# Weight decoding, attention factors and range checks moved to other steps in a fused RWKV and two-MLP kernel

## The chip, the cores and the metric

One core of a Trainium2 chip runs the whole program. The metric is the device time in microseconds (us), the median of three runs. The engines are named as in the profile: PE (TensorE) multiplies matrices, PEld is its weight load, DVE (VectorE), ACT (ScalarE) and POOL (GpSimd) work on elements, and SP issues the DMAs of this program. Each engine takes its instructions in the order in which the program lists them, so an instruction that waits holds up all that stand behind it on that engine.

## The reference

The input goes through a linear attention and then through two MLPs, all of it in float32:

```python
for t in range(S):                       # S = 768, per batch (4) and head (8), D = 48
    cur = einsum('bhd,bhe->bhde', u * kt, vt)
    y[:, :, t] = einsum('bhd,bhde->bhe', rt, state + cur)
    state = wt[..., None] * state + einsum('bhd,bhe->bhde', kt, vt)
x = y.transpose(0, 2, 1, 3).reshape(3072, 384)
h = x @ w_in;  g = h * clip(h + 3, 0, 6) / 6;  x = g @ w_out     # d_ff 2048
out = (x @ w_a) * (x @ w_b) @ w_out2                             # d_ff 1536
```

## The kernel before

The sequence is cut into 6 blocks of 128 positions; with 4 batches that makes 24 attention units (unit n is block n // 4, batch n % 4) and 6 token blocks of 512 tokens for the MLPs. Each fp32 product in the MLPs is made of three matmuls on rounded high and low parts (`mm3`, L471), so each operand is split into a high part (a rounding copy on ACT) and a low part (a subtraction on DVE).

Two hand-written schedules set the order. A list of tokens (`CFG["start"]`) runs units 0 to 7 and the first half (8 of 16 weight tiles) of the first layer for token block 0. Then `run` (L819 and on) goes through numbered steps s. Steps 8 to 95 are the rest of the first MLP: one step is one weight tile of one token block. Steps 8 to 15 are tiles 0 to 7 for block 1, steps 16 to 23 tiles 8 to 15 for block 0, steps 24 to 31 tiles 8 to 15 for block 1; then each of the blocks 2 to 5 has 16 steps. Steps 96 to 167 are the second MLP, 12 for each block; there the step is also counted as sb = s - 96.

In a step of the first MLP the engines get, in this order: the attention's element work that is due (`att_ew`, L378), the first product `h` on PE (`L1_pe`, L499) into one of two PSUM banks in turn, relu (`t`, L510, ACT), its product with h (`t<-t,h`, L514, DVE: below "mul"), `gh` (L518, ACT), `gl` (L523, DVE), the first decoding operation (L418, ACT), the split of the weight tile that was decoded two steps earlier (`w`: L462 on ACT, L465 on DVE), the second product `x2a` of step s - 2 on PE (`L2_pe`, L534), the rest of the decoding, then the attention's matmuls, its loads (`att_loads`, L396), and the loads and splits of the second MLP's input. Where a part of the first MLP ends (steps 7, 15, 23, ...), `L2_pe` also copies the three banks of `x2a` out: banks 0 and 2 on ACT (L560), bank 1 on DVE (L558). The next part's `x2a` writes the same three banks and waits for those copies.

**Decoding.** The weights come as 64-bit numbers. Tile i is loaded into `raw` (two buffers, 768 KB each; the copies of `x2a` take the same two buffers in turn) and made into fp32 by two scalings on ACT (L418, L427), a shift and a mask on DVE (L432, L436) and two additions on POOL (L443). `CFG["dec"]` names the steps in which tiles 8 to 15 are decoded; `w_step2` issues the load of the next tile right behind a tile's decoding. Tile f of these is needed by `h` at step f + 8. The second MLP's tiles are decoded at steps 80 to 104, one a step from step 94 on.

**Attention.** A unit goes through stages on consecutive steps. Stage 0 is `z` (L184), `c` (L192, L193), `s` (L197) and `k` (L206) on DVE: two scans of the decay, and the product of r and k with the factors (the "factor operation"). Stage 1 has PE transpose k (`T`, L251) and form r times k (`A`, L272); stage 3 has `Y` (L339), which reads r for the last time. `load_rkw` (L133) of unit n + 2 stands in stage 1 and fills the buffer of unit n, so SP waits there for unit n's `Y`. Units 8 to 11 (block 2) start at steps 17, 20, 23 and 26.

**Checks.** `check_load` and `check_unit` (L696, L702) reload each unit's decay and test its range: four operations on DVE (L707, L708, L709, L712), one unit on every second step from sb = 1 on. `check_sum` (L726) at sb = 62 adds the result up, and the program reads it at its end.

**Second MLP.** In each step `ab` (L475, two products into a pair of banks), `ta` on ACT (L597) and DVE (L598), `ph` (L601), `pl` (L602), and `oa` (L620) of step sb - 2. Its input comes back from DRAM (`x2_load`); for blocks 0 and 1 two halves are added (L576) and then split (L577 on ACT, L578 on DVE), all in `x2_split`. Block 1's loads stand in sb = 3, 5 and 7, and its splits in sb = 5, 7 and 9.

Of the kernel before, what the change touches and what calls it, by code (L numbers as in the profile page):

```python
# [12 lines left out]
ALU = mybir.AluOpType  # L13
# [6 lines left out]
NBLK = S // 128  # L20
NF1 = 16
NF2 = 12
# [16 lines left out]
    "off": (0, 3, 6, 9),  # L39
    "stage": (0, 1, 2, 3, 4, 5, 0, 2),  # L40
    "second": (17, 20, 23, 26),
    "dec": (10, 11, 13, 14, 16, 17, 19, 20),
    "late": (-16, -14, -12, -10, -8, -6, -4, -2, -1, 0, 1, 2, 3, 4, 5, 6, 7, 8),
    "heat": 13,
    "pool": (
# [27 lines left out]
def rwkv_moe_kernel(ctx: ExitStack, tc: tile.TileContext, rkw, nat, vst, wall, ub, ud, cst, out):  # L73
    nc = tc.nc
# [13 lines left out]
    x2p = [dr.tile([3, 128, 512], F32, name=f"x2p{j}", tag=f"x2p{j}") for j in range(2)]  # L88
# [30 lines left out]
    units = [(j, b) for j in range(NBLK) for b in range(B)]  # L119
# [13 lines left out]
    def load_rkw(n):  # L133
        j, b = units[n]
        if n in FIRST:
            t = spare([128, 1024], f"rkw{n}")
        else:
            t = ap_.tile([128, 1545], F32, name=f"rkw{n}", tag="rkw")
            U[n]["w"] = t[:, 1024:1545]
        if n == 0 or n in FIRST:  # L140
            nc.sync.dma_start(out=U[n]["w"], in_=rkw[b, j, :, 1024:1545])
            nc.sync.dma_start(out=t[:, 0:1024], in_=rkw[b, j, :, 0:1024])
        else:
            nc.sync.dma_start(out=t, in_=rkw[b, j])
        if 0 < n < N_DOT:
            get_nat(n)
        U[n]["rkw"] = t
# [7 lines left out]
    def load_nat(n):  # L155
        j, b = units[n]
        c = slice(2 * DM if n < N_DOT else 0, 3 * DM)
        nc.sync.dma_start(out=get_nat(n)[:, c], in_=nat[b, j, :, c])

    def load_vs(n):  # L160
        j, b = units[n]
        nc.sync.dma_start(out=U[n]["vs"], in_=vst[b, j].rearrange("p (a c d) -> p a c d", a=NP, c=2))
# [3 lines left out]
    def get_xT(j, nm):  # L166
        if (j, nm) not in xT:
            h = gp.tile([128, 3, 512], F32R, name=f"xh_{nm}{j}", tag="xh", bufs=2)
            l = gp.tile([128, 3, 512], F32R, name=f"xl_{nm}{j}", tag="xl", bufs=2)
            xT[(j, nm)] = (h, l)  # L170
        return xT[(j, nm)]
# [206 lines left out]
    def att_ew(n, stage):  # L378
        j = units[n][0]
        for a in {  # L380
            0: "zcsk", "d0": "d", "d1": "oO", 1: "u" if j else "", 2: "tm",
            3: "efh" if j < NBLK - 1 else "ef", "x": "x", 5: "HL",
        }.get(stage, ""):
            atom[a](n)
# [9 lines left out]
                nc.tensor.matmul(out=o, lhsT=wz[:, 0:128], rhs=wz, start=True, stop=True)  # L394

    def att_loads(n, stage):  # L396
        if stage == 1 and n + 2 < len(units):
            load_rkw(n + 2)
        elif stage == 3 and n + 2 < len(units):
            load_vs(n + 2)  # L400
        elif stage == 4 and n + 3 < len(units):
            load_nat(n + 3)

    raw = {}
# [94 lines left out]
    def L1_pe(s):  # L499
        (_, j, f, _, _), c0, c1 = part(s)  # L500
        h = bank(3 + slot(s) % 2, None, f"h{s}")[:, 0:c1 - c0]
        hb[s] = h
        xh, xl = xT[(j, "a")]
        w = W[f]
        mm3(h, [((w[:, 0, k * 128:(k + 1) * 128], w[:, 1, k * 128:(k + 1) * 128]), (xh[:, k, c0:c1], xl[:, k, c0:c1])) for k in range(3)])
# [20 lines left out]
    def L1_ew(s):  # L526
        L1_relu(s)
        L1_mul(s)

    def L1_ew2(s):  # L530
        L1_high(s)
        L1_low(s)
# [30 lines left out]
    def x2_load(j, k):  # L563
        e = gp.tile([128, 512], F32, name=f"x2r{j}_{k}", tag="t", bufs=3)
        nc.sync.dma_start(out=e, in_=x2d[j][k])
        raw["x2", j, k] = e
        if raw.get("parts") and j < 2:
            e = ap_.tile([128, 3 * DM], F32, name=f"x2q{j}_{k}", tag="nat", bufs=3)[:, 0:512]
            nc.sync.dma_start(out=e, in_=x2p[j][k])
            raw["x2p", j, k] = e  # L570

    def x2_split(j, k):
        h, l = get_xT(j, "b")
        e = raw.pop(("x2", j, k))
        if ("x2p", j, k) in raw:
            nc.vector.tensor_tensor(out=e, in0=e, in1=raw.pop(("x2p", j, k)), op=ALU.add)  # L576
        nc.scalar.copy(out=h[:, k], in_=e)  # L577
        nc.vector.tensor_tensor(out=l[:, k], in0=e, in1=h[:, k].bitcast(F32), op=ALU.subtract)  # L578

# [2 lines left out]
    def L3_pe(s):  # L582
        j, f = divmod(s, NF2)
        xh, xl = xT[(j, "b")]
        w = W[NF1 + f]
        r = []
        for q in range(2):
            o = bank((3, 4, 6, 7)[2 * (s % 2) + q], None, f"ab{s}_{q}")
            c = q * 384
            mm3(o, [((w[:, 0, c + k * 128:c + (k + 1) * 128], w[:, 1, c + k * 128:c + (k + 1) * 128]), (xh[:, k], xl[:, k])) for k in range(3)])  # L590
            r.append(o)
        ab[s] = r
# [48 lines left out]
    for n in range(FIRST_N, len(units)):  # L641
        j, i = divmod(n, 4)
        n0 = CFG["second"][i] if j == 2 else NF1 * (j - 1) + CFG["off"][i]
        a, b, c, d, x, h, d0, d1 = (n0 + k for k in CFG["stage"])
# [45 lines left out]
            w_ahead()  # L690

    UNITS = len(units)
    CHECK = max(NF2 * (NBLK - 1) + 2, 2 * UNITS + 4)
    chk = {}

    def check_load(n):  # L696
# [122 lines left out]
    def run(at, first, ew, fast):  # L819
        lag, end = [max(first - 1, 0), 0], NA + NBLK * NF2 - 1  # L820
        for s in range(first, end + 1):
            act = at.get(s, [])
            sb = s - NA
            for n, sg in act:
                ew(n, sg)
            if 0 <= s < NA:
                L1_pe(s)
            elif 0 <= sb < NBLK * NF2:
                L3_pe(sb)
            if 0 <= s < NA:  # L830
                L1_ew(s)
                L1_ew2(s)
            elif 0 <= sb < NBLK * NF2:
                L3_ew(sb)
            w_step1(s)
            w_step(s)
            while lag[0] <= min(s - 2, NA - 1):
                L2_pe(lag[0])
                lag[0] += 1
            while lag[1] <= (sb - 2 if s < end else sb):  # L840
                L4_pe(lag[1])
                lag[1] += 1
            if fast and sb == CHECK:
                check_sum()
            w_step2(s)
            for n, sg in act:
                att_pe(n, sg)
            if fast:
                for n, sg in act:
                    att_loads(n, sg)  # L850
                c, r = divmod(sb - 1, 2)
                if r == 0 and 0 <= c <= UNITS:
                    if c:
                        check_unit(c - 1)
                    if c < UNITS:
                        check_load(c)
                    else:
                        check_all()
            for j in range(NBLK):
                base = NA + NF2 * j - (12 if j else 13)  # L860
                for k in range(3):
                    if s == base + 3 + 2 * k:
                        x2_load(j, k)
                    if s == base + 5 + 2 * k:
                        x2_split(j, k)

# [110 lines left out]
```

## Time and profile before

| | |
|---|---|
| median of 3 runs | 1033.86 us (1032.52 to 1036.76) |
| the profiled execution | 1032.36 us |
| its span, first to last instruction | 1030.6 us, so 1.76 us lie around it |
| PE busy | 992.9 us (96%), 7135 matmuls |
| PE weight load busy | 816.9 us (79%) |
| DVE, ACT, POOL busy | 593.8 us (58%), 347.5 us (34%), 125.2 us (12%) |
| mean granted clock of PE | 0.986 |

The shares are means over very different stages. A table by stretch shows where PE stands idle, the timeline of PE shows which instruction it waited in front of, and the timelines of the other engines show what that instruction's releaser was doing. The granted clock is 1.00 at PE's upper level of 2.4 GHz and 0.50 at 1.2 GHz; a mean in between is a mixture of the two.

### The profile page before, as it was taken

How to read it: one execution, taken by the hardware profiler on the slowest of the kernel's cores; microseconds unless marked ns; L12 is line 12 of the kernel's file. 1: busy time of each engine (PE TensorE's matmuls, PEld its weight loads, DVE VectorE, ACT ScalarE, POOL GpSimd, SP SyncE). 2: the span in 40 equal slices, each digit the busy share in tenths (PEclk: the TensorE clock that was granted, in tenths of full speed). 3: DMA queues.
4: the chain of work that ended last, by engine and by line, in shares of the span. 5: the costliest groups of instructions: out<-in, count | busy, mean ns of one | idle time of the engine just before them, and what ended most of it. 6: DMA issues, size and time to landing. Idle time of an engine off the chain costs nothing.

```text
span 1030.6 us, 16913 instructions
## 1 busy us (share of the span) xinstructions
PE 992.9 (96%) x7135; PEld 816.9 (79%) x7135; DVE 593.8 (58%) x916; ACT 347.5 (34%) x582; POOL 125.2 (12%) x118
## 2 busy tenths in 40 slices
PE   8998977999999999999999997999999999999997
PEld 4776865777778788787887876888888888888886
DVE  8998687657655765663666677444444444322222
ACT  4364643333323323233556543222222222222211
POOL 1220243211211120210233331000000000000000
PEclk9999988999999999999999998999999999999999
DMA  7363432241321321220343441110110110100001
GB/s 280 126 232 130 161 104 89 85 135 65 110 99 57 101 86 65 90 101 1 102 145 121 160 157 43 56 50 30 62 42 22 62 41 21 52 11 1 32 1 34
DMA packets 30037, 86.64 MB, mean 84 GB/s; under 512 B 3456, under 2 KB 10880, under 8 KB 29952
## 3 DMA queue, kind: packets, MB, share of 16 engines
q1 hardware_dynamic: 29664, 85.37, 24.3%
q8 instruction: 58, 0.95, 0.4%
q14 instruction: 27, 0.22, 0.1%
q10 hardware_dynamic: 288, 0.10, 0.0%
HBM read 74.45 MB, written 11.01 MB: 83 GB/s over the span
## 4 chain that ended last, share of the span: by engine, by line
PE 43%; issue 33%; DVE 9%; POOL 6%; ACT 3%; DMA 2%; SPq 0%; POOLq 0%; ACTq 0%; DVEq 0%
PE ab L475 26%; PE oa L620 13%; DMA raw<-in_wall_dram 2%; POOL wa L443 2%; PE h L475 2%; PE x2a L544 1%; DVE w L465 1%; POOL nat L216 1%; POOL nat L215 1%; POOL nat L240 1%; DVE raw L436 1%; ACT raw L418 1%; DVE t L514 1%; DVE wa L432 1%; ACT w L462 1%
## 5 line engine op out<-in xcount | busy, mean ns | idle before, releaser
L475 PE MATMUL ab<-xh_b,w 128*128 128x512 f32 x864 | 227.4, 398 | 8.2 <-ACT w L462 5.9
L475 PEld LDWEIGHTS ab<-xh_b,w 128*128 128x128 f32 x864 | 162.3, 189 | 43.1 <-ACT w L462 6.2
L475 PE MATMUL h<-xh_a,w 128*128 128x512 f32 x576 | 159.0, 410 | 3.1 <-ACT w L462 1.3
L544 PE MATMUL x2a<-gh,w 128*128 128x512 f32 x576 | 154.9, 400 | 6.5 <-ACT x2e L560 6.1
L598 DVE TENSOR_TENSOR ta<-ab,ta 128x512 f32<-128x512 f32 x72 | 49.7, 690 | 190.6 <-PE ab L475 190.6
L544 PEld LDWEIGHTS x2a<-gh,w 128*128 128x128 f32 x576 | 108.9, 190 | 33.1 <-ACT x2e L560 6.5
L475 PEld LDWEIGHTS h<-xh_a,w 128*128 128x128 f32 x576 | 104.6, 190 | 29.0 <-DVE w L465 2.8
L475 PE MATMUL ab<-xl_b,w 128*128 128x512 f32 x432 | 124.8, 397 | 0.0
L510 ACT ACTIVATE t<-h,half 128x512 f32<-128x512 f32 x96 | 66.0, 688 | 156.3 <-PE h L475 156.2
L620 PE MATMUL oa<-w,ph 128*128 128x384 f32 x576 | 113.5, 338 | 0.0
L514 DVE SCALAR_TENSOR_TENSOR t<-t,h 128x512 f32<-128x512 f32 x96 | 65.6, 683 | 78.7 <-ACT t L510 78.7
L620 PEld LDWEIGHTS oa<-w,ph 128*128 128x128 f32 x576 | 103.1, 188 | 6.0
L523 DVE TENSOR_TENSOR gl<-t,gh 128x512 fp32r<-128x512 f32 x95 | 71.5, 753 | 60.6 <-ACT gh L518 60.6
L518 ACT CAST gh<-t 128x512 fp32r<-128x512 f32 x96 | 59.6, 621 | 123.7 <-DVE t L514 123.7
L475 PEld LDWEIGHTS ab<-xl_b,w 128*128 128x128 f32 x432 | 81.9, 189 | 20.1
L601 ACT CAST ph<-ta 128x512 fp32r<-128x512 f32 x72 | 44.7, 620 | 157.3 <-DVE ta L598 157.3
L597 ACT COPY ta<-ab 128x512 f32<-128x512 f32 x72 | 42.2, 586 | 159.0 <-PE ab L475 159.0
L443 POOL TENSOR_TENSOR wa<-wa,raw 128x384 int32<-128x384 int32 x59 | 68.4, 1179 | 223.8 <-DVE raw L436 174.8
L544 PE MATMUL x2a<-gl,w 128*128 128x512 f32 x288 | 85.9, 398 | 0.0
L602 DVE TENSOR_TENSOR pl<-ta,ph 128x512 fp32r<-128x512 f32 x72 | 54.8, 762 | 49.4 <-ACT ph L601 49.4
L475 PE MATMUL h<-xl_a,w 128*128 128x512 f32 x288 | 83.2, 397 | 0.0
L544 PEld LDWEIGHTS x2a<-gl,w 128*128 128x128 f32 x288 | 54.6, 190 | 13.6 <-DVE gl L523 0.3
(88 smaller groups left out, 1028.7 us busy)
## 6 DMA issues: line engine op xcount, KB each, us to landing
raw<-in_wall_dram SPq DMA_DIRECT2D x34, 768.0 KB, 4.6
rkw<-in_rkw_dram SPq DMA_DIRECT2D x21, 772.5 KB, 4.4
nat<-in_nat_dram SPq DMA_DIRECT2D x16, 576.0 KB, 3.9
cw<-in_rkw_dram SPq DMA_DIRECT2D x24, 260.5 KB, 2.8
x2d<-x2e SPq DMA_DIRECT2D x18, 256.0 KB, 2.4
x2r<-x2d SPq DMA_DIRECT2D x18, 256.0 KB, 3.0
out_dram<-oe SPq DMA_DIRECT2D x24, 192.0 KB, 2.0
vs<-in_vst_dram SPq DMA_DIRECT2D x22, 192.0 KB, 4.6
```

The lines of the kernel that those rows point to most:

```text
L443: eng.tensor_tensor(out=a[:, c], in0=a[:, c], in1=t[:, c, 0], op=ALU.add)
L475: nc.tensor.matmul(out=o, lhsT=lt, rhs=rt, start=(i == 0), stop=(i == 3 * n - 1))
L510: nc.scalar.activation(out=t, in_=hb[s], func=ACTF.Relu, bias=half, scale=1.0 / 6.0)
L514: nc.vector.scalar_tensor_tensor(out=t, in0=t, scalar=1.0, in1=hb.pop(s), op0=ALU.min, op1=ALU.mult)
L518: nc.scalar.copy(out=gh, in_=G["t", s])
L523: ve(f"l{s}").tensor_tensor(out=gl, in0=G.pop(("t", s)), in1=G[s][0].bitcast(F32), op=ALU.subtract)
L544: nc.tensor.matmul(out=acc1[i][k][:, c0:c1], lhsT=w[:, e, 384 + k * 128:512 + k * 128], rhs=rt, start=(first and e == 0 and rt is gh), sto ...
L597: nc.scalar.copy(out=t, in_=a)
L598: nc.vector.tensor_tensor(out=t, in0=bb, in1=t, op=ALU.mult)
L601: nc.scalar.copy(out=gh, in_=t)
L602: nc.vector.tensor_tensor(out=gl, in0=t, in1=gh.bitcast(F32), op=ALU.subtract)
L620: nc.tensor.matmul(out=acc2[j][b][:, 0:384], lhsT=lt[:, b * 128:(b + 1) * 128], rhs=rt, start=(f == 0 and rt is wh and lt is ph), stop=(la ...
```

## The change

Tiles 8 to 15 are decoded at steps 9 to 16, one a step. The factor operation `k` goes from stage 0 to stage 1, ahead of `u` (L309), and the load of unit n + 2's r, k and w goes from stage 1 to stage 3. The checks start at sb = 12 and end at sb = 60. The addition of the two halves of x2 becomes a function of its own and stands one step ahead of the split.

```diff
-    "dec": (10, 11, 13, 14, 16, 17, 19, 20),
+    "dec": (9, 10, 11, 12, 13, 14, 15, 16),
...
-            0: "zcsk", "d0": "d", "d1": "oO", 1: "u" if j else "", 2: "tm",
+            0: "zcs", "d0": "d", "d1": "oO", 1: "ku" if j else "k", 2: "tm",
...
-        if stage == 1 and n + 2 < len(units):
+        if stage == 3 and n + 2 < len(units):
             load_rkw(n + 2)
-        elif stage == 3 and n + 2 < len(units):
             load_vs(n + 2)
...
+    def x2_sum(j, k):
+        if ("x2p", j, k) in raw:
+            e = raw["x2", j, k]
+            nc.vector.tensor_tensor(out=e, in0=e, in1=raw.pop(("x2p", j, k)), op=ALU.add)
+
     def x2_split(j, k):
         h, l = get_xT(j, "b")
         e = raw.pop(("x2", j, k))
-        if ("x2p", j, k) in raw:
-            nc.vector.tensor_tensor(out=e, in0=e, in1=raw.pop(("x2p", j, k)), op=ALU.add)
...
-    CHECK = max(NF2 * (NBLK - 1) + 2, 2 * UNITS + 4)
+    CHECK = max(NF2 * (NBLK - 1) + 2, 2 * UNITS + NF2 + 2)
...
-                c, r = divmod(sb - 1, 2)
+                c, r = divmod(sb - NF2, 2)
...
+                    if s == base + 4 + 2 * k:
+                        x2_sum(j, k)
```

Three places show what moves. The first is ACT in steps 9 to 11, where `x2e0` are the copies of the first part's banks and `raw8` is weight tile 8. Before, from step 9's `gh` on:

```order
L518 CAST gh9_1439<-t9_1436 128x512
L560 COPY x2e0_1452<-x2a0_0_860 128x512
L560 COPY x2e0_1452<-x2a0_2_862 128x512
L510 ACTIVATE t10_1469<-h10_1459,half_85 128x512
L518 CAST gh10_1472<-t10_1469 128x512
L418 ACTIVATE raw8_1407<-raw8_1407 128x768
L427 ACTIVATE raw8_1407<-raw8_1407 128x768
L510 ACTIVATE t11_1507<-h11_1497,half_85 128x512
```

The same place after the change:

```order
L517 CAST gh9_1439<-t9_1436 128x512
L417 ACTIVATE raw8_1407<-raw8_1407 128x768
L559 COPY x2e0_1453<-x2a0_0_860 128x512
L559 COPY x2e0_1453<-x2a0_2_862 128x512
L426 ACTIVATE raw8_1407<-raw8_1407 128x768
L509 ACTIVATE t10_1478<-h10_1468,half_85 128x512
L517 CAST gh10_1481<-t10_1478 128x512
L417 ACTIVATE raw9_1466<-raw9_1466 128x768
L426 ACTIVATE raw9_1466<-raw9_1466 128x768
L509 ACTIVATE t11_1516<-h11_1506,half_85 128x512
```

Tile 8's first scaling now stands ahead of the two bank copies, and tile 9's in step 10, ahead of step 11's relu.

The second is DVE where unit 8 begins (step 17): `zp8`, `pc8`, `seed` are `z`, `c` and `s`, the operation that writes `rkw8` is `k`, and `x2e1` is the copy of the second part's bank 1. Before:

```order
L436 SCALAR_TENSOR_TENSOR raw12_1632<-raw12_1632 128x768
L184 SCALAR_TENSOR_TENSOR zp8_1701<-rkw8_1268,ones_rev_87 128x520
L192 TENSOR_SCALAR pc8_1703<-zp8_1701 128x8
L193 RECIPROCAL seed_88<-pc8_1703 128x8
L197 SCALAR_TENSOR_TENSOR zp8_1701<-rkw8_1268,seed_88 128x519
L206 TENSOR_TENSOR rkw8_1268<-rkw8_1268,zp8_1701 128x1024
L514 SCALAR_TENSOR_TENSOR t17_1720<-t17_1720,h17_1710 128x512
L523 TENSOR_TENSOR gl17_1725<-t17_1720,gh17_1723 128x512
L558 COPY x2e1_1737<-x2a1_1_1478 128x512
L432 TENSOR_SCALAR wa13_1745<-raw13_1699 128x768
```

After the change:

```order
L435 SCALAR_TENSOR_TENSOR raw15_1694<-raw15_1694 128x768
L184 SCALAR_TENSOR_TENSOR zp8_1732<-rkw8_1268,ones_rev_87 128x520
L192 TENSOR_SCALAR pc8_1734<-zp8_1732 128x8
L193 RECIPROCAL seed_88<-pc8_1734 128x8
L197 SCALAR_TENSOR_TENSOR zp8_1732<-rkw8_1268,seed_88 128x519
L513 SCALAR_TENSOR_TENSOR t17_1750<-t17_1750,h17_1740 128x512
L522 TENSOR_TENSOR gl17_1755<-t17_1750,gh17_1753 128x512
L464 TENSOR_TENSOR w14_1757<-wa14_1689,w14_1757 128x768
L557 COPY x2e1_1769<-x2a1_1_1487 128x512
L206 TENSOR_TENSOR rkw8_1268<-rkw8_1268,zp8_1732 128x1024
```

What stands ahead of unit 8 is now the mask of the last tile (15) instead of tile 12's, `k` stands behind step 17's products, and no decoding follows.

The third is DVE in sb = 5 and 6 of the second MLP (`raw32`, `raw26` are weight tiles, `cw1` is a unit's decay under check, `x2r1_0` the first third of block 1's input). Before:

```order
L436 SCALAR_TENSOR_TENSOR raw32_5939<-raw32_5939 128x768
L707 TENSOR_REDUCE chk_m_5879<-cw1_5884 128x1
L708 TENSOR_REDUCE chk_m_5879<-cw1_5884 128x1
L709 SCALAR_TENSOR_TENSOR cw1_5884<-cw1_5884,ones_rev_87 128x520
L712 COPY chk_p_5878<-cw1_5884 128x8
L576 TENSOR_TENSOR x2r1_0_5886<-x2r1_0_5886,x2q1_0_5888 128x512
L578 TENSOR_TENSOR xl_b1_5999<-x2r1_0_5886,xh_b1_5998 128x512
L598 TENSOR_TENSOR ta6_6027<-ab6_1_6017,ta6_6027 128x512
```

After the change:

```order
L435 SCALAR_TENSOR_TENSOR raw32_5929<-raw32_5929 128x768
L580 TENSOR_TENSOR xl_b1_5984<-x2r1_0_5876,xh_b1_5983 128x512
L600 TENSOR_TENSOR ta6_6011<-ab6_1_6001,ta6_6011 128x512
L604 TENSOR_TENSOR pl6_6015<-ta6_6011,ph6_6014 128x512
L464 TENSOR_TENSOR w25_6019<-wa25_5924,w25_6019 128x768
```

The four check operations are gone from between the mask and step 6's product, and the addition has gone to the step before.

## Rows read from the trace of the kernel before

**Rows 1.** Windows: us, PE, PEld, DVE, ACT, POOL busy (count), PEclk, DMA share, GB/s

```profile
33.00:39.00 6.00, 4.80 (x62) 3.10 (x63) 5.97 (x10) 1.37 (x6) 2.09 (x2) 0.72 0.26 99
169.00:186.00 17.00, 9.66 (x87) 7.28 (x87) 9.39 (x16) 6.68 (x10) 4.90 (x5) 0.70 0.13 50
618.90:631.60 12.70, 6.57 (x21) 4.80 (x20) 9.68 (x14) 5.87 (x9) 3.21 (x3) 0.73 0.19 62
203.00:553.00 350.00, 350.00 (x3051) 279.77 (x3051) 217.01 (x355) 126.66 (x202) 51.40 (x51) 1.00 0.26 90
646.40:1023.00 376.60, 376.60 (x1793) 327.95 (x1792) 142.98 (x226) 82.34 (x141) 0.00 (x0) 1.00 0.10 32
```

**Rows 2.** PE timeline: start us, us, what, count [idle before <-releaser]

```profile
135.54 1.56 PE L475 MATMUL h<-xh_a,w 128*128 128x512 f32 x6
139.76 1.57 PE L475 MATMUL h<-xh_a,w 128*128 128x512 f32 x6
148.09 2.50 PE L544 MATMUL x2a<-gh,w 128*128 128x512 f32 x5 [6.06 <-ACT x2e L560]
175.44 1.98 PE L272 MATMUL A<-rkw 48*64 48x64 f32 x32 [5.40 <-DVE nat L349]
```

**Rows 3.** DVE and ACT timelines at step 17; SP's waits from 160 to 170 us

```profile
139.53 1.23 DVE L184 TENSOR_TENSOR_SCAN zp<-rkw,ones_rev 128x520 f32<-128x520 f32 x1
143.69 1.83 DVE L206 TENSOR_TENSOR rkw<-rkw,zp 128x1024 f32<-128x1024 f32 x1
145.44 0.68 DVE L514 SCALAR_TENSOR_TENSOR t<-t,h 128x512 f32<-128x512 f32 x1
147.47 1.05 ACT L560 COPY x2e<-x2a 128x512 f32<-128x512 f32 x2
...
SPq L144 <- PE Y L339: 11.6, 1, 11.6
```

**Rows 4.** DVE, ACT, POOL and SP timelines, a decoding at step 13 and behind

```profile
121.76 0.69 DVE L514 SCALAR_TENSOR_TENSOR t<-t,h 128x512 f32<-128x512 f32 x1 [0.55 <-ACT t L510]
126.88 0.68 DVE L514 SCALAR_TENSOR_TENSOR t<-t,h 128x512 f32<-128x512 f32 x1
123.01 0.90 ACT L418 ACTIVATE raw<-raw 128x768 f32<-128x768 f32 x1
127.04 2.04 POOL L443 TENSOR_TENSOR wa<-wa,raw 128x384 int32<-128x384 int32 x2 [7.24 <-DVE raw L436]
129.10 4.32 SPq L410 DMA_DIRECT2D raw<-in_wall_dram  x2
```

**Rows 5.** Tile raw from 88 to 200 us, and SP's issue of tile 8

```profile
DMA to landing us min/median/max: 4.2/4.2/8.1
99.60 0.46 SPq L410 DMA_DIRECT2D raw<-in_wall_dram  x1
```

**Rows 6.** PE timeline of the second MLP's first steps, columns as in rows 2

```profile
566.38 1.57 PE L475 MATMUL ab<-xh_b,w 128*128 128x512 f32 x6
606.15 1.67 PE L475 MATMUL ab<-xh_b,w 128*128 128x512 f32 x6 [1.72 <-ACT ta L597]
624.94 0.79 PE L475 MATMUL ab<-xh_b,w 128*128 128x512 f32 x1 [5.86 <-ACT w L462]
646.36 1.57 PE L475 MATMUL ab<-xh_b,w 128*128 128x512 f32 x6
652.70 1.56 PE L475 MATMUL ab<-xh_b,w 128*128 128x512 f32 x6
```

**Rows 7.** DVE timeline there: a check, an addition, two products

```profile
601.08 0.69 DVE L707 TENSOR_REDUCE chk_m<-cw 128x1 f32<-128x521 f32 x1
604.28 0.68 DVE L576 TENSOR_TENSOR x2r<-x2r,x2q 128x512 f32<-128x512 f32 x1
606.25 0.68 DVE L598 TENSOR_TENSOR ta<-ab,ta 128x512 f32<-128x512 f32 x1
611.57 0.69 DVE L598 TENSOR_TENSOR ta<-ab,ta 128x512 f32<-128x512 f32 x1
```

## The prediction, written before the changed kernel ran

> **What bounds the kernel now.** I read the table by stretch first. From 203 to 553 us and from 646 to 1023 us PE is busy for the whole stretch at a granted clock of 1.00, its 2.4 GHz level [rows 1]: nothing that other engines do faster there can shorten the run. What can be won lies in the rows of that table in which PE is not full, 169 to 186 us and 618.9 to 631.6 us, and in the two waits of PE's timeline that are nearest to them. So I took PE's timeline next, for the instruction that waited and its releaser, then the timelines of DVE, ACT and SP, for what the releaser had been doing.
>
> First stall: the first `x2a` of step 16 waits 6.06 us, until 148.09, for ACT's copies of the part before [rows 2]. ACT makes them behind step 17's `gh`, and that needs step 17's mul on DVE, which stands behind unit 8's `z`, `c`, `s` and `k` [rows 3]. Second stall: at 175.44 `A` of unit 9 had waited 5.40 us for a bank that DVE frees [rows 2]; DVE stood behind the decoding of tile 15, whose load SP issued late, since it stood for 11.6 us at the load of unit 10 until unit 8's `Y` was done [rows 3]. Third: in the second MLP's first steps PE waits 1.72 us for `ta` and 5.86 us for a weight split [rows 6], while DVE does decoding, a check and an input addition in one step [rows 7].
>
> **The checks and the addition.** Steps sb = 2 to 13 ran from 566.38 to 652.70, 86.3 us for 12 steps; the last of them, undisturbed, took 6.34 [rows 6], and 12 of these are 76.1. So 10.2 us are lost there, the slow clock behind the longest wait (0.73 in the window) included [rows 1]. Is DVE fast enough without the checks? From step 6's product to step 7's, with a decoding and a split but no check, it needs 5.32 us (611.57 - 606.25), and a check takes from 601.08 to 604.28, 3.2 us [rows 7]. So a step without a check leaves DVE 1.0 us below PE's 6.34, and with one it is 2.2 us over; the checks stand on sb = 3, 5, 7 and 9 of this stretch. The addition (0.68) and the split of x2 now fall into different steps, so that neither makes a step longer than about 6.0, and ACT finds the sum ready instead of waiting for it. I take the whole 10.2. The ends: nothing, if the load waits of that stretch alone can hold `ta` and the splits back, and 10.2; my reason for the upper end is that the loop is then shorter than PE's step in each step, so a lag shrinks instead of growing.
>
> Where do the checks go? Each adds 3.2 us of DVE on every second step of sb = 14 to 60. DVE is busy 143 of 376.6 us there, most of the checks included [rows 1], and PE's step is 6.34; a product of `ab` has two steps until its banks are written again. Cost 0; without that cover it would be 24 times 3.2, 77 us of DVE, of which PE would see what exceeds its steps. The last check is ten steps before the end.
>
> **`k` and the load of r, k, w.** `k` (1.83 us here, where POOL works beside it) goes from ahead of mul to the step behind, where `T` stands two products later: about 4 us after the step's start, while `k` can start about 1 us after it. Where PE is full the move is worth 0 [rows 1]; at step 17 it takes its 1.83 us out of the chain, which is counted below. The load waited for `Y` before and waits for it now; what is gone is SP standing still in between. The transfer for unit n + 2 starts at the same time. Alone: 0.
>
> **The decoding.** Here I expect a new loss that pays for what is won. Three sums.
>
> *DVE and ACT.* In a step with a decoding and a split the time from mul to mul is 126.88 - 121.76 = 5.12 us [rows 4]; PE's step is 139.76 - 135.54 = 4.22 us [rows 2]. Before, two such steps were followed by a lighter one. Now steps 11 to 16 are all of that kind.
>
> *Loads.* Tile 10's first scaling starts at 123.01, its additions end at 127.04 + 2.04, and SP issues the load that goes into this buffer at 129.10 [rows 4]. It lands 4.2 us later [rows 5]: 10.3 to 10.4 us from scaling to scaling of one buffer, 5.2 us a tile with two. So both chains are slower than 4.22, and I go by the load chain, the longer one.
>
> *The start.* Tile 8's load is issued at 99.60 and is the one that lands after 8.1 us, at 107.7 [rows 5]. Its first scaling now stands ahead of the copies of the banks in ACT's queue, so these start at 108.5, and PE loses 1.0 us. The rest of the decoding takes 6 us, as from 123.01 to 129.1 [rows 4], so tile 9's load leaves at 113.7, with tile 10's right behind it: between 4.2 alone and 8.1 in a crowd I take 5.0, near the single load since only two fly. Tile 9's scaling starts at 118.7 with ACT's later relus behind it. Tile 9 has no split in its step, which makes its decoding about 1 us shorter, so tile 11 follows 9.3 us later, and tiles 13 and 15 after 10.4 each: 118.7, 128.0, 138.4, 148.8. PE waits about 1 us in each step from 13 to 18 for the bank that a late mul frees, and step 18's `h` starts near 148.2, not at 139.76.
>
> Tile 15's mask ends 3.9 us behind its scaling (126.88 - 123.01 [rows 4]), at 152.7. Then `z`, `c`, `s` take 143.69 - 139.53 = 4.16 us beside POOL, mul starts at 156.9, and the copies 2.0 us later (147.47 - 145.44 [rows 3]; a tile's split stands in between now where a scaling stood), PE 0.6 behind them. So `x2a` starts near 159.5 instead of 148.09, 11.4 us later. Bank 1's copy stands behind a split on DVE and may add some tenths, which I leave to the range.
>
> From there on no tile is decoded. The second stall goes: in 169 to 186 PE is idle 7.34 us, its 9.66 us of work at a mean clock of 0.70 hold 2.9 us more than at 1.00 [rows 1], 10.2 together. The load that held SP comes behind all tiles now. What is late next is mul of step 20, behind unit 9's scans, by about 1.5 us, and no PE instruction needs it for 4. So this half costs 11.4 - 10.2 = 1.2 us. Its bounds: single loads at 4.2 and a shorter mask give back about 4; loads at 8.1 in the chain of four (3 times 3.9) cost 11.7 more.
>
> **Sum.** -10.2 + 1.2 = -9.0 us on the profiled execution's 1032.36: 1023.4. The median of the runs shown is 1.5 above that execution, so for a median I forecast 1033.86 - 9.0 = 1024.9 us, 0.9% faster. About 0.5%, 5.2 us, can be told from no change.
>
> **The rivals.**
> *The decoding keeps pace.* If the load waits are hidden, `x2a` starts where it did and only the second stall goes: 10.2 beside the second MLP's 10.2, so 1013.5. For it: at step 13 ACT's scaling waited for no load [rows 4]. Against: before, one step in three had no decoding, and these let the chain catch up. 0.12.
>
> *The second MLP's waits stay in part,* since a late weight load and not a check holds DVE: at least the 5.86 us wait with its clock loss, 7.9, would remain, 1032.8. Against it stands the 5.32. 0.10.
>
> *Crowded loads.* Each of the chain's loads takes 8.1: 1036.6. It needs other traffic, and SP issues nothing else there. 0.06.
>
> *The clock falls in the stretch of short waits.* The mechanism: PE idles about 1 us in each of seven steps (11 to 18), the granted clock falls to 1.2 GHz, a step's 4.22 us become 8.44, and PE is then slower than the 5.2 us chain. Price: up to 3.2 us a step, 22.5 in all, 1047.4. It costs from a mean clock below 4.22 / 5.2 = 0.81, and the change is a loss from 9.0 / 7 = 1.3 us a step, a clock near 0.65. For it: from 33 to 39 us PE was 80% busy and the mean clock 0.72 [rows 1], as full as PE would be here. Against: the wait of 1.72 us at 606.15 was followed by six matmuls in 1.67 us, full speed [rows 6]. The Trainium skill, "TensorE: Matmul & The Clock Gate", section "A second HAM failure mode: psum-queue depth-cycling", speaks for this rival: it tells of a kernel in which frequent short idles of PE between groups of matmuls let the clock swing between its two levels. By that rule the time would be near 1047, by the row at 606.15 1024.9; the row is the same kernel with the same matmuls, so I give it the larger weight. 0.06.
>
> **Numbers.** The forecast has 0.66. Its own range is 1020 to 1030. With the rivals the range 1016 to 1033 leaves out the kept pace (0.12), the crowded loads' and the clock's upper ends, and little else. Faster by over 0.5% (below 1028.7): nearly all of the forecast and the kept pace, 0.76. Within 0.5% (to 1039.0): the partial second stall, crowded loads and the forecast's upper tail, 0.18. Slower: the clock, 0.06.
>
> **What would show it.** Right: no wait of PE above 1 us between 566 and 652 us of the old count; ACT waiting for tile loads in front of its first scalings at steps 9 to 16, 8 us or more in all; PE's waits near 1 us in steps 13 to 18; one wait of about 9 us ahead of step 16's `x2a`, and none ahead of `A` of unit 9. Wrong: a time below 1016 with that wait gone, or a second MLP that still waits for a split.

## The result, and the profile after

The changed kernel takes 1025.07 us (median of 5 runs, 1019.32 to 1027.54) against 1034.26 us (5 runs, 1032.52 to 1037.49) for the kernel before: a ratio of 0.9899, with a 95% interval of 0.9861 to 0.9936. Faster, then, by 0.6% to 1.4%; 1024.9 us had been forecast.

The profiled execution took 1026.16 us, its span 1024.3. It began badly: step 9's `h`, ahead of which the change touches nothing, starts 4.2 us later than in the profile of before (last section). So I compare stretches, each from the start of the first matmul of one product to that of another in PE's timeline: from step 9's `h` to step 24's, on to the second MLP's first `ab`, and sb = 2 to 13 of the second MLP. Us:

| kernel | step 9 to 24 | step 9 to second MLP | sb = 2 to 13 |
|---|---|---|---|
| before | 90.56 | 451.29 | 86.32 |
| changed | 91.14 | 451.87 | 75.85 |

Steps 9 to 24 are 0.58 us longer, the second MLP's stretch 10.47 us shorter, and sb = 0 and 1 lose 0.64 (13.29 to 12.65). The rest is equal: with the 4.2 us of the opening these add up to the 6.3 us between the two spans (1030.6 and 1024.3). Without the opening the change is worth 10.5 us, a little more than the 9.2 between the medians.

The table by stretch of the changed kernel, which answers to [rows 1], columns as there:

```profile
102.00:142.00 40.00, 34.39 (x145) 26.10 (x144) 23.17 (x29) 20.60 (x31) 8.84 (x9) 1.00 0.52 188
152.00:169.00 17.00, 7.54 (x26) 5.14 (x28) 14.57 (x18) 7.81 (x13) 7.60 (x6) 0.70 0.13 50
169.00:186.00 17.00, 17.00 (x210) 13.61 (x211) 11.24 (x20) 4.96 (x8) 2.82 (x3) 1.00 0.18 59
566.00:652.00 86.00, 86.00 (x407) 74.43 (x406) 50.44 (x65) 40.61 (x63) 19.82 (x18) 1.00 0.32 112
646.40:1017.00 370.60, 370.60 (x1765) 322.78 (x1764) 154.69 (x244) 80.72 (x139) 0.00 (x0) 1.00 0.12 36
```

The second MLP is full from its start. The hole that lay at 169 to 186 us is gone, and a deeper one lies ahead of it, at 152 to 169 us, with the slow clock in it (0.70). DVE is busy 155 us in the last row, where it was 143 for a stretch of nearly the same length: the checks, now beside a full PE. PE's timeline says what the hole is:

```profile
125.80 1.67 PE L474 MATMUL h<-xh_a,w 128*128 128x512 f32 x6 [1.93 <-DVE t L513]
131.04 1.67 PE L474 MATMUL h<-xh_a,w 128*128 128x512 f32 x6 [0.76 <-DVE t L513]
...
152.46 1.67 PE L474 MATMUL h<-xh_a,w 128*128 128x512 f32 x6 [0.94 <-DVE t L513]
163.62 1.22 PE L543 MATMUL x2a<-gh,w 128*128 128x512 f32 x2 [8.79 <-ACT x2e L559]
165.06 2.08 PE L543 MATMUL x2a<-gh,w 128*128 128x512 f32 x4 [0.22 <-DVE x2e L557]
...
185.25 1.15 PE L272 MATMUL A<-rkw 48*64 48x64 f32 x32
```

Six short waits ahead of `h` (three shown), and 8.79 us ahead of step 16's `x2a` instead of 6.06. `A` of unit 9 had waited 5.40 us [rows 2] and waits no more.

### The profile page after: what moved, and what is told of

Same layout as the page of the kernel before. It is cut to its first block, busy times and chain, and to the rows that moved or that the text cites. A ratio compares the mean times of both kernels' runs of the same rounds, so it can differ in the third digit from the quotient of the medians.

```text
span 1024.3 us, 16915 instructions
## 1 busy us (share of the span) xinstructions
PE 994.0 (97%) x7133; PEld 817.8 (80%) x7135; DVE 590.3 (58%) x916; ACT 347.4 (34%) x582; POOL 120.4 (12%) x118
## 4 chain that ended last, share of the span: by engine, by line
PE 85%; DVE 7%; ACT 2%; DMA 1%; issue 1%; POOL 0%; DVEq 0%; ACTq 0%; POOLq 0%; SPq 0%
PE ab L474 30%; PE h L474 17%; PE x2a L543 17%; PE oa L622 15%; PE Y L339 2%; PE A L272 2%; DMA raw<-in_wall_dram 1%; PE K L294 1%; DVE raw L435 1%; DVE w L464 1%; DVE t L513 1%; PE T L251 1%; PE X L356 1%; ACT raw L417 1%; DVE wa L431 1%
## 5 line engine op out<-in xcount | busy, mean ns | idle before, releaser
L543 PEld LDWEIGHTS x2a<-gh,w 128*128 128x128 f32 x576 | 108.6, 190 | 37.5 <-ACT x2e L559 10.2
L522 DVE TENSOR_TENSOR gl<-t,gh 128x512 fp32r<-128x512 f32 x95 | 75.5, 795 | 60.5 <-ACT gh L517 60.5
L442 POOL TENSOR_TENSOR wa<-wa,raw 128x384 int32<-128x384 int32 x59 | 65.3, 1126 | 207.0 <-DVE raw L435 138.7
```

Source lines behind the costliest of these rows:

```text
L442: eng.tensor_tensor(out=a[:, c], in0=a[:, c], in1=t[:, c, 0], op=ALU.add)
L522: ve(f"l{s}").tensor_tensor(out=gl, in0=G.pop(("t", s)), in1=G[s][0].bitcast(F32), op=ALU.subtract)
L543: nc.tensor.matmul(out=acc1[i][k][:, c0:c1], lhsT=w[:, e, 384 + k * 128:512 + k * 128], rhs=rt, start=(first and e == 0 and rt is gh), sto ...
```

## The experiments

### The checks alone

```diff
-    CHECK = max(NF2 * (NBLK - 1) + 2, 2 * UNITS + 4)
+    CHECK = max(NF2 * (NBLK - 1) + 2, 2 * UNITS + NF2 + 2)
...
-                c, r = divmod(sb - 1, 2)
+                c, r = divmod(sb - NF2, 2)
```

> The kernel before with the checks alone moved to sb = 12 to 60; the addition of x2 stays inside its split. My theory: a check's 3.2 us of DVE on every second step are the loss, so the steps sb = 2 to 13 fall from 86.3 us to between 76 and 78, all else stays, and the whole is 9 to 10 us faster than before. Rival: the addition that stands ahead of the split (ACT waits for it) is the cause of the 5.9 us wait; then more than 6 of the 10.2 us stay and the whole is at most 4 us faster.

Measured: 1024.24 us (4 runs; before on the same chip 1035.89, 19 runs), ratio 0.9889 (0.985 to 0.9928). sb = 2 to 13 take 75.85 us, as in the changed kernel; steps 9 to 24 stay (90.38). One part of the change gives the whole gain, as far as these intervals can tell. In sb = 0 and 1 one wait of 0.34 us stays, so the 0.64 us there are not the checks'.

### The addition alone

```diff
+    def x2_sum(j, k):
+        if ("x2p", j, k) in raw:
...
+                    if s == base + 4 + 2 * k:
+                        x2_sum(j, k)
```

> The kernel before with the addition of x2 alone moved one step ahead of its split; checks, decoding, k and loads stay. My theory: the checks are the cost, so sb = 2 to 13 stay at 84 to 87 us (86.3 before), and sb = 0 to 2 lose at most the 0.6 us that the changed kernel is shorter there. Rival: the addition in front of the split is what ACT and then PE wait for; then the 5.9 us wait goes and sb = 2 to 13 take 80 us or less.

Measured (one run, 1034.11 us): sb = 2 to 13 take 84.04 us, sb = 0 and 1 12.66. Steps 9 to 24, the same instructions as before, read 91.96 against 90.56: such a reading carries about 1.5 us of scatter. PE's timeline from 555 to 660 us holds only these waits:

```profile
626.05 0.80 PE L475 MATMUL ab<-xh_b,w 128*128 128x512 f32 x1 [5.03 <-ACT w L462]
627.12 2.50 PE L475 MATMUL ab<-xh_b,w 128*128 128x512 f32 x5 [0.27 <-DVE w L465]
```

The 1.72 us wait for `ta` [rows 6] went with the addition, the long one stayed, and the matmuls behind it are still slow (2.50 us for five). The checks hold that one. sb = 0 and 1 take 12.66 us here, as in the changed kernel: their 0.64 us are the addition's.

### The decoding alone

```diff
-    "dec": (10, 11, 13, 14, 16, 17, 19, 20),
+    "dec": (9, 10, 11, 12, 13, 14, 15, 16),
```

> The kernel before with the decoding alone moved to steps 9 to 16; the factor operation and the loads of r, k and w stay. My theory: step 16's first x2a starts as late as in the changed kernel or 1.8 us later, since the factor operation stands ahead of step 17's mul again (about 161 us counted as before), and the second stall is gone, since no tile's load stands behind the load of unit 10 any more; steps 9 to 24 take 92 to 94 us against 90.6, the whole is 1 to 3 us slower than before. Rival: the early load of r, k and w makes the second stall, whatever the decoding; then it stays and steps 9 to 24 take about 102 us, the whole is 11 to 13 us slower.

Measured: ratio 1.001 (0.9986 to 1.0034, 10 runs), steps 9 to 24 92.72 us. Step 16's `x2a` starts at 170.41 us behind a wait of 10.68 us, which is 161.5 counted as before (step 9 lies 8.95 us later here). The second stall is gone although the load of r, k and w stands where it stood: the rival falls. Alone the decoding wins nothing.

### `k` and the load of r, k and w alone

```diff
-            0: "zcsk", "d0": "d", "d1": "oO", 1: "u" if j else "", 2: "tm",
+            0: "zcs", "d0": "d", "d1": "oO", 1: "ku" if j else "k", 2: "tm",
...
-        if stage == 1 and n + 2 < len(units):
+        if stage == 3 and n + 2 < len(units):
             load_rkw(n + 2)
...
```

> The kernel before with the factor operation one stage later and the load of r, k and w two stages later, the decoding as before. My prediction's sentence: alone these are worth 0; at most the 1.8 us of the factor operation come out of the chain to step 16's x2a, so steps 9 to 24 take 88.7 to 90.6 us. Rival: SP no longer stands at the load of unit 10, tile 15's load leaves up to 11.6 us earlier, and the second stall (10.2 us with its slow clock) goes without any decoding moved; then steps 9 to 24 take 78.5 to 81 us and the whole is 9.5 to 12 us faster.

Measured: ratio 0.9978 (0.9956 to 1.0, 10 runs), steps 9 to 24 87.97 us. The wait ahead of step 16's `x2a` fell from 6.06 to 4.18 us, about `k`'s 1.83 [rows 3]. The second stall stayed, now ahead of `T` of unit 9. The profile names no releaser for it ("issue"), but `T` reads what `k` writes, and it starts at 175.30, 0.09 us behind `k`'s end (173.49 + 1.72). Three timelines there, of PE, ACT and DVE:

```profile
175.30 0.98 PE L251 MATMUL T<-cst_sb,rkw 112*128 112x112 f32 x4 [5.46 <-issue]
```

```profile
170.35 0.91 ACT L417 ACTIVATE raw<-raw 128x768 f32<-128x768 f32 x1
```

```profile
170.48 0.69 DVE L522 TENSOR_TENSOR gl<-t,gh 128x512 fp32r<-128x512 f32 x1 [0.69 <-ACT gh L517]
171.29 0.56 DVE L431 TENSOR_SCALAR wa<-raw 128x768 int32<-128x768 int32 x1
172.08 0.96 DVE L435 SCALAR_TENSOR_TENSOR raw<-raw 128x768 int32<-128x768 int32 x1 [0.23 <-ACT raw L426]
172.95 0.61 DVE L349 TENSOR_TENSOR nat<-Y,nat 128x192 f32<-128x192 f32 x2
173.49 1.72 DVE L206 TENSOR_TENSOR rkw<-rkw,zp 128x1024 f32<-128x1024 f32 x1
```

and ACT's scaling of the same tile in the kernel before:

```profile
172.46 0.88 ACT L418 ACTIVATE raw<-raw 128x768 f32<-128x768 f32 x1 [1.84 <-DMA raw<-in_wall_dram]
```

Before, tile 15's scaling waited 1.84 us for its load. With SP free it waits for nothing, but `k`, out of the unit's first step, now stands ahead of `T` and takes 1.72 us there. One was bought with the other, and the rest of the stall was not the load here: DVE works through without a gap but for 0.69 and 0.23 us. No run moves the load without `k`, so what the load alone would win, up to its 1.84 us, stays open.

### The changed kernel with the old decoding

```diff
-    "dec": (9, 10, 11, 12, 13, 14, 15, 16),
+    "dec": (10, 11, 13, 14, 16, 17, 19, 20),
```

> The changed kernel with the decoding back at steps 10, 11, 13, 14, 16, 17, 19 and 20. My theory that the decoding costs what it wins: steps 9 to 24 take about 89 to 91 us, as before and as changed, and the time is that of the changed kernel within 2 us. Rival: the load's move alone frees the second stall, and the one-a-step decoding only costs its 11 us; then steps 9 to 24 take 78.5 to 81 us and this kernel is 9 to 12 us faster than the changed one, near 1013 to 1015 us.

Measured: 1022.51 us (4 runs), ratio 0.9856 (0.981 to 0.9902); steps 9 to 24 take 88.00 us, to the second MLP 448.73, and the wait ahead of step 16's `x2a` is 4.17 us. The second stall there:

```profile
179.96 0.98 PE L251 MATMUL T<-cst_sb,rkw 112*128 112x112 f32 x4 [5.45 <-issue]
```

Neither theory: this stall stays, against the rival, and yet the stretch is 3.1 us shorter than the changed kernel's and 1.0 below the 89 that I expected at the least. The whole times cannot tell the two kernels apart (0.9856 and 0.9899, and the intervals overlap). The stretches can, with some care: up to step 24 this kernel has the instructions of the run of `k` and the load alone, which read 87.97, and three pairs of kernels that differ by the decoding alone have the same sign: 92.72 against 90.56 and 91.14 against 88.00 for steps 9 to 24 and, with unit 8 later (below), 449.65 against 447.99 to the second MLP. Moving the decoding was a small loss, some 2 us, beside the other parts.

### Unit 8 one step later

```diff
-    "second": (17, 20, 23, 26),
+    "second": (18, 21, 24, 26),
```

> The changed kernel with unit 8 begun one step later (units 8 to 11 at steps 18, 21, 24 and 26 instead of 17, 20, 23 and 26). My theory: of the 8.8 us that step 16's first x2a waits, 4.0 are unit 8's z, c and s ahead of step 17's mul on DVE and the rest is the decoding's lag; the wait falls to 4 to 5 us and steps 9 to 24 take 85.5 to 87.5 us instead of 91.1. Rival: DVE's work as a whole is the limit there, so that z, c and s cost the same one step later, as a wait ahead of T of unit 8 or of step 20's h; then steps 9 to 24 stay within 1.5 us of 91.1.

Measured (one run, 1020.93 us): steps 9 to 24 take 86.76 us. The wait is 5.06 us, with 1.25 more for DVE's copy of bank 1:

```profile
156.42 1.22 PE L543 MATMUL x2a<-gh,w 128*128 128x512 f32 x2 [5.06 <-ACT x2e L559]
158.89 2.08 PE L543 MATMUL x2a<-gh,w 128*128 128x512 f32 x4 [1.25 <-DVE x2e L557]
```

So `z`, `c` and `s` are 3.7 of the 8.8 us, of which bank 1's copy takes 1.0 back (1.25 instead of 0.22). Some of unit 10's matmuls now lie behind step 24, so the net is read to the second MLP: 449.65 against 451.87 us, 2.2 less, not far above the scatter of one reading.

### The low part one place earlier

```diff
...
+        if s < 24 and raw.get("parts"):
+            while pend and pend[0][0] <= s - 1:
+                lows.append(pend.pop(0)[1])
+                w_high(lows[-1])
...
                 L1_ew(s)
+                w_low_due()
                 L1_ew2(s)
```

> The changed kernel in which a tile of steps 9 to 16 is rounded one step after its decoding (not two) and its low part is formed one place earlier, between step s's mul and gl on DVE, where DVE stood 0.69 us for gh. The loop on DVE from mul to mul was 5.3 us; without the 0.69 and the 0.2 us wait for ACT's rounding it is 4.4. Theory that DVE's loop bounds the steps 11 to 16: mul to mul falls to 4.4 to 4.7 us (the upper figure is the load chain, 10.5 us for two tiles less the 1.1 us by which the mask comes sooner), the short waits of PE before h go from 5.8 us in all to under 3, step 16's x2a starts 4 us or more earlier, and steps 9 to 24 take 85 to 88 us. Rival, my prediction's sentence: the loads bound it at 5.2 us a tile; then mul to mul stays at 5.2 or more, ACT's first scaling waits for loads at 0.5 us or more a step, and steps 9 to 24 stay at 90 to 91 us.

Measured (one run, 1025.86 us): mul to mul 5.5 us, steps 9 to 24 91.25 us. The theory's numbers failed. DVE in the changed kernel, one turn:

```profile
130.31 0.68 DVE L513 SCALAR_TENSOR_TENSOR t<-t,h 128x512 f32<-128x512 f32 x1
131.68 1.41 DVE L522 TENSOR_TENSOR gl<-t,gh 128x512 fp32r<-128x512 f32 x1 [0.69 <-ACT gh L517]
133.36 0.96 DVE L464 TENSOR_TENSOR w<-wa,w 128x768 fp32r<-128x768 f32 x1 [0.28 <-ACT w L461]
134.36 0.56 DVE L431 TENSOR_SCALAR wa<-raw 128x768 int32<-128x768 int32 x1
134.83 0.95 DVE L435 SCALAR_TENSOR_TENSOR raw<-raw 128x768 int32<-128x768 int32 x1
```

and in this experiment:

```profile
130.28 0.68 DVE L513 SCALAR_TENSOR_TENSOR t<-t,h 128x512 f32<-128x512 f32 x1
130.88 1.46 DVE L464 TENSOR_TENSOR w<-wa,w 128x768 fp32r<-128x768 f32 x1
132.26 1.52 DVE L522 TENSOR_TENSOR gl<-t,gh 128x512 fp32r<-128x512 f32 x1
133.71 0.55 DVE L431 TENSOR_SCALAR wa<-raw 128x768 int32<-128x768 int32 x1
134.95 0.96 DVE L435 SCALAR_TENSOR_TENSOR raw<-raw 128x768 int32<-128x768 int32 x1 [0.70 <-ACT raw L426]
```

The two gaps (0.69 and 0.28) are filled as meant, but the low part beside POOL's additions takes 1.46 instead of 0.96 us, and the mask waits 0.70 for ACT's second scaling, which stands behind a rounding that waits for POOL. What DVE won was given back on two other engines. POOL's two additions, now beside the low part and `gl`, take 2.7 instead of 2.0 us, so each load leaves later, and ACT's first scalings of tiles 11 to 15 wait 0.39 to 0.52 us for theirs. That is near the rival's figures: this run alone speaks for the loads.

### Four loads left out

```diff
+            if raw.get("parts") and 11 < i < NF1:
+                raw[i] = raw["keep", i] = raw["keep", i - 2]
+                return
```

> The changed kernel without the loads of tiles 12 to 15 (they are decoded out of what tiles 10 and 11 left in the two buffers, so the weights of these four tiles are not the reference's); every other instruction stays. Theory that the chain of DVE, ACT and POOL bounds the decoding with one tile a step: the scalings of tiles 12 to 15 still start 5.2 to 5.4 us apart (5.3 in the changed kernel), PE's waits before h in steps 14 to 18 stay near 0.8 us each, and step 16's x2a waits 8 to 9 us as before. Rival, my prediction's sentence that the loads are the longer chain: without them the scalings come 5.1 us apart or less, the waits shrink, and x2a starts 1 us or more earlier in its stretch.

Measured (one run, 1027.23 us; steps 9 to 24 90.66): ACT's first scalings of tiles 10, 12 and 15 there:

```profile
127.40 0.91 ACT L421 ACTIVATE raw<-raw 128x768 f32<-128x768 f32 x1
...
137.98 0.91 ACT L421 ACTIVATE raw<-raw 128x768 f32<-128x768 f32 x1
...
153.69 0.91 ACT L421 ACTIVATE raw<-raw 128x768 f32<-128x768 f32 x1
```

(153.69 - 137.98) / 3 = 5.24 us a tile, against 5.34 in the changed kernel (tile 12 at 136.94, tile 15 at 152.96). PE's waits ahead of `h` from 132 to 154 us stay at 0.76 to 0.86 us, and `x2a` waits 8.73. Counted from step 9, `x2a` starts 1.17 us earlier than in the changed kernel, as the rival asked; but 0.74 of that is there at step 12's mul, before tile 12's load, the first that is left out, would have been issued. The loads are worth 0.1 us a tile; without them the loop over DVE, ACT and POOL still takes 5.24. Taken with the run before, the two chains are of one length: where the loads were gone the loop stayed, and where the loop's gaps were filled ACT waited for the loads.

### Towards a faster version

Both old decoding steps and the later units (the two diffs above together):

> The changed kernel with the decoding at its old steps (10, 11, 13, 14, 16, 17, 19, 20) and units 8 to 11 at steps 18, 21, 24 and 26. With the old decoding alone two waits were left, 4.17 us ahead of step 16's x2a and 5.45 us ahead of T of unit 9, and steps 9 to 24 took 88.0 us. Theory that both waits come from a unit's scans standing in one step with a decoding or with the copies: the first goes to under 0.5 us, the second to under 3, and steps 9 to 24 take 79 to 84 us. Rival: DVE's work as a whole is the limit; then a wait of 4 us or more appears at another place and steps 9 to 24 take 86.5 us or more.

Measured (one run, 1020.3 us): steps 9 to 24 85.13 us, to the second MLP 447.99. The wait ahead of `x2a` is 0.37 us; 4.20 us stand ahead of `T` of unit 8 and 4.79 ahead of step 22's `h`. The first half of the theory held; the second wait moved and did not shrink.

In addition, a unit's scans, `k` and `u` between mul and gl:

```diff
+            mid = fast and 16 < s < 32
             for n, sg in act:
-                ew(n, sg)
+                if not (mid and sg in (0, 1)):
+                    ew(n, sg)
...
                 L1_ew(s)
+                for n, sg in act:
+                    if mid and sg in (0, 1):
+                        ew(n, sg)
                 L1_ew2(s)
```

> The changed kernel with the decoding at its old steps, units 8 to 11 at steps 18, 21, 24 and 26, and in steps 17 to 31 the scans, k and u of a unit on DVE between the step's mul and gl, where DVE stood 0.69 us for gh, and not ahead of mul. With the first two edits alone two waits were left, 4.2 us ahead of T of unit 8 and 4.8 us ahead of step 22's h, and the stretch from step 9 to the second MLP took 448.0 us. Theory that DVE's time as a whole is what is left there: what is filled in (0.69 us in each of the steps 18, 19, 21 and 22) comes off the two waits, which fall to 2 to 3.5 us each, and the stretch takes 444 to 447 us. Rival: a wait's place is set by its own chain, T's by z, c, s and k, which are not shorter and begin 0.7 us later; then T's wait stays at 4 us or more and the stretch takes 447.5 us or more.

Measured (one run, 1018.1 us): to the second MLP 447.39 us, a gain within the scatter; `T` waits 4.73, step 22's `h` 4.1. The rival's wait, the theory's direction, neither clearly.

Then `k` behind the scans again, and the split ahead of them:

```diff
-            0: "zcs", "d0": "d", "d1": "oO", 1: "ku" if j else "k", 2: "tm",
+            0: "zcsk", "d0": "d", "d1": "oO", 1: "u" if j else "", 2: "tm",
...
+                if mid and any(sg == 0 for _, sg in act):
+                    w_step(s)
```

> The edits of the last run (old decoding steps, units at 18, 21, 24 and 26, a unit's work between mul and gl), and in addition k right behind the scans again, as before the change, and in a step where a unit begins the weight tile's split ahead of the scans. In the last run PE waited 4.7 us ahead of T of unit 8 and 4.1 us ahead of step 22's h, the latter for a split. Theory that each of these waits is a chain on DVE that can be shortened by order alone: k no longer stands behind gl, a split and the next mul (3.5 us), so T waits 1 to 2 us; the split stands ahead of 4 us of scans, so h waits under 0.5 us; with the slow clock behind each the stretch from step 9 to the second MLP takes 438 to 443 us against 447.4, and the time is 1009 to 1014 us, 2.0 to 2.4 per cent faster than before. Rival: DVE's time as a whole is the limit; then 3 us or more of wait appears at other places, and the stretch takes 446 us or more.

Measured: 1017.21 us (6 runs, 1011.8 to 1020.08; before 1034.66, 11 runs), ratio 0.9823 (0.9788 to 0.9858). To the second MLP 446.66 us: the expected 438 to 443 was missed and the rival's figure came. Windows and PE's timeline:

```profile
142.00:152.00 10.00, 6.65 (x27) 4.92 (x27) 9.54 (x11) 3.99 (x7) 5.62 (x4) 0.98 0.58 213
152.00:169.00 17.00, 16.24 (x174) 12.77 (x175) 13.92 (x20) 8.36 (x12) 7.49 (x7) 0.81 0.08 28
```

```profile
152.62 0.98 PE L251 MATMUL T<-cst_sb,rkw 112*128 112x112 f32 x4 [3.83 <-issue]
...
175.98 0.79 PE L474 MATMUL h<-xh_a,w 128*128 128x512 f32 x1 [1.09 <-ACT w L461]
```

Step 22's wait went, and 1.09 us stand ahead of step 23's `h` now (the second line). `T` still waits 3.83 us, and in the ten us up to it DVE is busy 9.54, which speaks for the rival: order alone moves little there. The kernel is faster than the changed one: the interval of its ratio and that one's (0.9861 to 0.9936) don't meet. Against the kernels of the two runs before it, of which there is one run each, nothing is shown.

## Why the prediction was right, point by point

**The checks: -10.2 forecast, -10.47 measured,** and shown by the checks alone. The argument that DVE's loop is 1.0 us shorter than PE's step without a check held: no wait is left. Of the addition, which the prediction counted in the same sum, 0.64 us in sb = 0 and 1 remain; it removes the short `ta` wait, but the checks alone remove that too.

**Checks elsewhere, 0:** from sb = 14's first `ab` to the end the kernels take 377.9 us, before (652.70 to 1030.6) and after (646.39 to 1024.3), and PE is full there. The move of `k` costs nothing where PE is full either: step 24 to the second MLP takes 360.73 us in both.

**Step 16's `x2a`: 11.4 us later forecast; 163.62 - 148.09 - 4.22 = 11.3 measured,** the 4.22 being the later start of step 9. The place, the queue and the size were right, and so, nearly, were the short waits: near 1 us forecast in steps 13 to 18, 0.76 to 1.93 measured. **The step that failed is the sentence "I go by the load chain, the longer one."** ACT waited for loads twice, 7.0 us in all, and only at the start; it was to be 8 us or more through steps 9 to 16:

```profile
111.63 0.91 ACT L417 ACTIVATE raw<-raw 128x768 f32<-128x768 f32 x1 [1.18 <-DMA raw<-in_wall_dram]
...
122.37 0.91 ACT L417 ACTIVATE raw<-raw 128x768 f32<-128x768 f32 x1 [5.83 <-DMA raw<-in_wall_dram]
...
126.31 0.91 ACT L417 ACTIVATE raw<-raw 128x768 f32<-128x768 f32 x1
```

From then on the tiles follow each other at 5.3 us without a load wait, and without loads at 5.24. I had 5.12 for the loop and 5.2 for the loads, two numbers 2% apart, and chose by the larger. The loads were sized rightly: tile 10's scaling starts at 126.31, tile 12's load is issued at 132.56 and lands 4.2 us later, 10.4 us for two tiles. The loop was sized too short. Its 5.12 were read in a step of the kernel before in which `gl` ran alone and DVE then waited for ACT's rounding:

```profile
123.14 0.69 DVE L523 TENSOR_TENSOR gl<-t,gh 128x512 fp32r<-128x512 f32 x1 [0.69 <-ACT gh L518]
124.66 0.96 DVE L465 TENSOR_TENSOR w<-wa,w 128x768 fp32r<-128x768 f32 x1 [0.83 <-ACT w L462]
```

With a decoding in every step `gl` runs beside POOL's additions, 1.41 us, and the shorter wait behind it (0.28) gives back only a part. That the time came out although the wrong chain was chosen is luck: the two are nearly equal. The agreement of the medians within 0.2 us (1024.9 and 1025.07) is luck too, since the five runs spread over 8 us and by stretches the change is worth 10.5 us and not 9.0.

**The second stall, -10.2:** it went, and the decoding's move took it, as the run of the decoding alone shows. The reason given was half wrong: "DVE stood behind the decoding of tile 15, whose load SP issued late." The lateness was 1.84 us; with SP free and `k` moved the stall stayed at 5.46, with no load wait in it. It is DVE's work in steps 20 and 21 that PE waits for there.

**`k` and the load, 0 alone, with 1.83 us counted in the chain:** 1.88 us came off the wait, steps 9 to 24 lost 2.6. Not seen was that `k` would stand ahead of unit 9's `T`, where the old decoding still fell.

**The first half, +1.2: +0.58 measured,** and the signs of its two parts are now known: -2.6 for `k` and the load (against the kernel before), +3.1 for the decoding (against the changed kernel with the old one), each within some 1.5 us. For the first, the two readings with it, 87.97 and 88.00, lie below all three without it, 90.38 to 91.96; for the second, the three pairs stand above.

**Of the rivals** none came. The decoding did not keep pace (short waits from 1.93 down to 0.76 us, a wait of 8.79). No wait stayed in the second MLP. The loads were not crowded: from issue to landing 4.1 us at the least, 4.3 in the middle, 7.8 at most. And the clock held: PE was busy 34.39 of 40 us from 102 to 142 with its short waits, and the granted clock there is 1.00. The Trainium skill's "TensorE: Matmul & The Clock Gate", section "A second HAM failure mode: psum-queue depth-cycling", which was named beside that rival, tells of short idles between groups that make the clock swing; this trace does not show it at 0.76 to 1.93 us a step.

## What to carry to other kernels

Find which engine's queue is short of time before moving work inside it: here checks that had a full PE to hide behind were worth 1%, while reorderings within DVE's crowded steps mostly turned one wait into the next. When an operation leaves one chain, look for the chain that it enters; `k` left `x2a`'s and entered `T`'s. When two chains are within a few per cent of each other, say that both bound, and test by taking one away. And read an operation's time in a step that has the neighbours it will have: `gl` was priced alone and ran beside POOL.

## What the hardware showed that was not expected

**The opening varies.** The same instructions up to step 8 ran with different clocks. The table by stretch, two of the rows that differ, first of the kernel before, then of the changed one:

```profile
10.00:20.00 10.00, 8.25 (x102) 5.08 (x99) 9.83 (x13) 6.02 (x13) 2.04 (x2) 1.00 0.97 363
...
40.00:50.00 10.00, 9.71 (x186) 8.04 (x183) 9.96 (x20) 4.97 (x15) 3.37 (x3) 1.00 0.22 65
```

```profile
10.00:20.00 10.00, 8.07 (x93) 6.01 (x91) 9.83 (x13) 4.82 (x9) 1.48 (x2) 0.75 0.96 349
...
40.00:50.00 10.00, 9.35 (x132) 7.81 (x134) 8.40 (x16) 2.14 (x8) 3.37 (x3) 0.61 0.15 34
```

The first `h` starts at 48.31 us in one and 52.98 in the other, and between 48.1 and 57.6 over all profiles of the study. That is as large as most effects here, and why stretches were compared. Why the clock differs there is not shown.

**DVE slows beside POOL, but not for every operation.** `gl` takes 0.69 us alone and 1.41 beside POOL's additions, the weight's low part 0.96 and 1.46; mul takes 0.68 either way. The Trainium skill, "SBUF — State Buffer", section "Who interferes with whom", says that a DVE instruction with two SBUF inputs contends with a GpSimd instruction that reads SBUF. The trace agrees for these three: `gl` and the low part have two such inputs, mul takes `h` from PSUM. The loss is 0.7 us on each `gl`, not a whole addition of 1.0 us. Two other operations show that the sentence is not all of it. A unit's `c` (128x8, one such input) takes 0.17 us alone and 0.79 or more beside POOL. And the check's scan, with two such inputs, took its 1.23 us beside the additions as it does alone; there POOL paid, with 3.04 us for a pair that took 2.01 in the step before, without a check. POOL in the kernel before, with the scan running from 602.28 to 603.51:

```profile
601.29 3.04 POOL L443 TENSOR_TENSOR wa<-wa,raw 128x384 int32<-128x384 int32 x2 [4.59 <-DVE raw L436]
```
